# The first expert product of 39 couples as seven block products in place of eight

## The chip, the core and the metric

The kernel runs on one core of one Trainium2 chip. Its engines work side by side, each through its own list of instructions in order: TensorE (PE) for matmuls, VectorE (DVE), ScalarE (ACT), GpSimd (POOL), and SyncE (SP), which here issues most of the DMAs. POOL issues the indirect DMAs (gathers and scatters by a list of row numbers) and does tensor work between them. The metric is the device time of one execution in microseconds (us); lower is better. A change is faster or slower for us when it moves that time by more than about 0.2%.

## What is computed

A batch of 8 sequences of 2496 rows of 256 numbers passes through a filter in the frequency domain, and every row is then treated by one of eight experts. Cut to what matters:

```python
X = np.fft.rfft(x, axis=1)
Yr, Yi = Xr @ w_r - Xi @ w_i + b_r, Xr @ w_i + Xi @ w_r + b_i
Y = soft_threshold(Yr, 0.01) + 1j * soft_threshold(Yi, 0.01)
x = np.fft.irfft(Y, n=2496, axis=1).reshape(19968, 256)

e_idx = argmax(x @ w_gate)                      # one expert for each row
for e in range(8):
    h = np.maximum(x[e_idx == e] @ w1[e], 0)    # first product, 256 -> 1024
    out[e_idx == e] = gate * (h @ w2[e])        # second product, 1024 -> 256
```

The change touches the line of the first product, `x @ w1[e]`, for a part of the rows.

## The kernel before

**Numbers in two halves.** Every f32 operand of a product is kept as two f16 tensors, a high and a low part, and a product is three f16 matmuls into the same PSUM bank: high by high, high by low, low by high. So a tile of weights or tokens has an index `v` of 0 or 1, and ACT makes the high part and DVE (or POOL) the low part of each.

**Phases.** The transform runs sequence by sequence (stages called stage1, stage2, mix, inverse, stage4). Its rows go to a table `yd` in DRAM, with the gate values. Rows are sorted to experts by counting, and from then on the work is by tiles of 128 rows. Two tiles of one expert are a couple. `T_A` = 64 tiles (32 couples) come from the first four sequences; they are the first phase of the experts and overlap the last sequences of the transform. `T_2` = 78 tiles (39 couples) are the second phase, and with them, spread evenly, go `T_M` = 18 mixed tiles, each of which has 64 rows of one expert and 64 of another. `BLOCKS` holds the order of couples and mixed tiles, `SEQ` that of tiles, `POS` the place of a tile in it.

**The path of a tile.** `gathers`: POOL fetches its rows with an indirect DMA (L1485). `tokens`: DVE finds the largest value and a power of two as scale (L438 to L449, L1507), ACT makes the high part (L1512), DVE the low part (L1513); SP turns both round with a transposing DMA into `eT` (L1526). `up`: the first product, 48 matmuls for a couple in four PSUM banks of 128 x 512 (L1617). ACT writes the high part of the positive values to `hh` (L1627), DVE the low part (L1628), and the bank is free. `down`: the second product, 24 matmuls a tile (L1581). ACT scales the result (L1597), POOL scatters it to `out` with an indirect DMA (L1600).

**Weights.** They lie in DRAM (`wd`) as f16 halves, 8192 columns an expert, half for each product. `W` holds three places for couples and two for mixed tiles. `fetch` and `half_fetch` load a place when its next couple has another expert; the DMA is issued every time but has a condition, and does nothing when the expert is the same.

**What sets the order.** Nothing is scheduled on the chip. When the program is built, a planner (class `Issue`) plays all the work through as generators: `yield "P", r, d, f` asks for engine P (PE), with due time `r` and planned duration `d`, and `f` writes the instruction. A free engine takes the waiting piece with the earliest due time. `yield slots[...]` waits for a buffer, `yield "name", t` for an event. Only the order that comes out goes to the chip, engine by engine; there the engines wait for each other by semaphores. The constants at the head of the file are due times and offsets. The planner counts an indirect DMA as 1.0 us of POOL.

`blocks_` starts a `block` for each couple or mixed tile, 5.6 us of due time a tile. In `tokens`, a tile waits for the first product of the tile `AHEAD` places before it.

## Time and profile before

| | us |
|---|---|
| runs (three): median, lowest, highest | 1423.33, 1422.81, 1424.46 |
| the profiled execution, as timed | 1422.78 |
| its span, from first to last instruction | 1421.0 |
| PE, DVE, ACT, POOL busy in it | 1390.6, 986.2, 738.9, 650.5 |
| first product of couples (L1617), 3408 matmuls, busy | 389.2 |
| second product of couples (L1581), 3408 matmuls, busy | 391.0 |

[...] What a matmul costs in a row of them is the distance of their starts: the span of a group of them, from its start to the start of the next group. Rows of the profile name the line of the program, the engine, the operation, the output and the inputs by tile name, shapes, and counts. In rows of instructions in order of time the first number is the start, the second the time taken, and the bracket the idle time of that engine just before, with what ended it. In rows of stretches each engine has its busy time and its number of instructions; PEclk is the granted clock of TensorE.

### The profile page before, as it was taken

How to read it: one execution, taken by the hardware profiler on the slowest of the kernel's cores; microseconds unless marked ns; L12 is line 12 of the kernel's file. 1: busy time of each engine (PE TensorE's matmuls, PEld its weight loads, DVE VectorE, ACT ScalarE, POOL GpSimd, SP SyncE). 2: the span in 40 equal slices, each digit the busy share in tenths (PEclk: the TensorE clock that was granted, in tenths of full speed). 3: DMA queues.
4: the chain of work that ended last, by engine and by line, in shares of the span. 5: the costliest groups of instructions: out<-in, count | busy, mean ns of one | idle time of the engine just before them, and what ended most of it. 6: DMA issues, size and time to landing. Idle time of an engine off the chain costs nothing.

```text
span 1421.0 us, 40860 instructions
## 1 busy us (share of the span) xinstructions
PE 1390.6 (98%) x15696; PEld 1237.5 (87%) x15696; DVE 986.2 (69%) x2849; ACT 738.9 (52%) x1401; POOL 650.5 (46%) x733
## 2 busy tenths in 40 slices
PE   7999999999999999899999999999999999999996
PEld 5998989898988888789998888999989999999996
DVE  5888877789999888668998774555455545554541
ACT  4877687778677765343333344434444434434431
POOL 3464645564567663334455634343343334333311
PEclk9999999999999999999999999999999999999999
DMA  8699989898988898786353373554644565555440
GB/s 212 166 212 230 205 226 207 214 212 224 217 203 188 201 227 190 196 253 174 97 158 78 88 178 80 135 142 128 164 107 103 135 168 132 135 137 139 126 106 23
DMA packets 285997, 231.54 MB, mean 163 GB/s; under 512 B 239246, under 2 KB 248080, under 8 KB 279167
## 3 DMA queue, kind: packets, MB, share of 16 engines
q1 hardware_dynamic: 270377, 187.02, 54.1%
q0 software_dynamic: 15424, 41.90, 12.7%
q8 instruction: 123, 2.02, 0.6%
q14 instruction: 73, 0.60, 0.1%
HBM read 286.72 MB, written 58.52 MB: 243 GB/s over the span
## 4 chain that ended last, share of the span: by engine, by line
PE 83%; DVE 6%; issue 5%; DMA 2%; POOL 2%; ACT 1%; SPq 1%; POOLq 0%; DVEq 0%; ACTq 0%
PE ps L1617 27%; PE ps L1581 26%; PE ps L823 11%; PE ps L715 5%; PE ps L793 3%; PE ps L919 3%; PE ps L853 3%; DMA x<-in_x 1%; PE ps L964 1%; PE ps L758 1%; POOL out L1600 1%; PE ps L817 1%; PE ps L599 1%; PE ps L1385 1%; DVE z L839 1%
## 5 line engine op out<-in xcount | busy, mean ns | idle before, releaser
L1617 PE MATMUL ps<-eT,wbuf 128*128 128x256 f16 x3408 | 389.2, 273 | 3.6 <-DMA wbuf<-wd 3.6
L1581 PE MATMUL ps<-wbuf,hh 128*128 128x256 f16 x3408 | 391.0, 273 | 0.0
L1617 PEld LDWEIGHTS <-wbuf 128*128 128x128 f16 x3408 | 331.6, 98 | 43.7 <-DMA wbuf<-wd 3.8
L1581 PEld LDWEIGHTS <-hh 128*128 128x128 f16 x3408 | 329.0, 98 | 41.9 <-issue 3.8
L1628 DVE SCALAR_TENSOR_TENSOR hh<-ps,hh 128x512 f16<-128x512 f32 x284 | 196.0, 690 | 225.7 <-ACT hh L1627 224.6
L1600 POOL DMA_INDIRECT out<-o,sidx x160 | 166.0, 1038 | 372.7 <-ACT o L1597 351.6
L1627 ACT ACTIVATE hh<-ps 128x512 f16<-128x512 f32 x284 | 169.5, 597 | 231.7 <-PE ps L1617 229.8
L823 PE MATMUL ps<-whl,xt 128*128 128x256 f16 x1920 | 222.6, 273 | 0.0
L1485 POOL DMA_INDIRECT yg<-yd,gidx x160 | 158.2, 989 | 138.7 <-DVE yhl L1513 82.9
L823 PEld LDWEIGHTS <-xt 128*128 128x128 f16 x1920 | 187.8, 98 | 30.9 <-issue 0.6
L1597 ACT ACTIVATE o<-ps,facs 128x256 f32<-128x256 f32 x160 | 75.7, 473 | 178.5 <-PE ps L1581 169.3
L1512 ACT ACTIVATE yhl<-yg,ys 128x256 f16<-128x256 f32 x160 | 80.8, 506 | 66.9 <-DVE ysi L449 31.7
L715 PE MATMUL ps<-f1t,x 117*128 117x120 f32 (+1 forms) x704 | 90.3, 282 | 9.2 <-DMA x<-in_x 7.8
L715 PEld LDWEIGHTS ps<-f1t,x 117*128 117x128 f32 (+1 forms) x704 | 85.6, 197 | 12.6 <-issue 9.1
L843 POOL TENSOR_TENSOR zhl<-z,zhl 128x512 f16<-128x512 f32 x64 | 75.6, 1182 | 30.8 <-ACT zhl L841 15.4
L1513 DVE SCALAR_TENSOR_TENSOR yhl<-yg,ys,yhl 128x256 f16<-128x256 f32 x160 | 78.9, 509 | 14.1 <-ACT yhl L1512 13.9
L842 POOL CAST zhl<-z 128x512 f16<-128x512 f32 x54 | 34.1, 631 | 107.7 <-DVE z L839 76.6
L838 ACT ACTIVATE zhl<-ps,sc 128x512 f32<-128x512 f32 x80 | 54.8, 686 | 39.1 <-PE ps L823 32.1
L1122 POOL TENSOR_TENSOR wsp<-wr,wsp 128x512 f16<-128x512 f32 x58 | 70.7, 1219 | 4.8
L1628 DVE SCALAR_TENSOR_TENSOR lategt<-ps,lategt 128x512 f16<-128x512 f32 x36 | 24.8, 688 | 65.8 <-ACT lategt L1627 65.8
L839 DVE SCALAR_TENSOR_TENSOR z<-ps,zhl 128x512 f32<-128x512 f32 x80 | 54.6, 684 | 20.7 <-ACT zhl L838 19.4
L919 PE MATMUL ps<-bdt,f4t 120*117 120x512 f16 x264 | 68.8, 379 | 0.0
(236 smaller groups left out, 2113.6 us busy)
## 6 DMA issues: line engine op xcount, KB each, us to landing
wbuf<-wd SPq DMA_DIRECT2D x142, 1024.0 KB
latebt<-wd SPq DMA_DIRECT2D x36, 1024.0 KB
latebdt<-wd SPq DMA_DIRECT2D x36, 1024.0 KB
yd<-yt SPq DMA_DIRECT2D x120, 158.4 KB
x<-in_x SPq DMA_DIRECT2D x106, 156.0 KB
wr<-in_moe_w SPq DMA_DIRECT2D x32, 512.0 KB
wd<-wsp SPq DMA_DIRECT2D x64, 256.0 KB
yg<-yd,gidx POOLq DMA_INDIRECT x160
```

What stands on the lines that cost most here:

```text
L715: T.matmul(pv[:, dh, :, m * j:m * j + m], xs[:k, j0 + j, 128 * dh:128 * dh + 128], fw, start=True, stop=True)
L823: T.matmul(yp[:, 256 * j:256 * j + 256], xt_[:, v, 2 * dh + j, 64 - 64 * u:192 - 64 * u], whl[:, dh, vw, 256 * u:256 * u + 256], start=Fal ...
L919: T.matmul(pt[:P3], w, src[:, :, :, vb_], start=(n == 0), stop=(n == 2))
L1485: yield "G", r + 5.6 * POS[t] - 30, 1.0, lambda: G.indirect_dma_start(out=yg, out_offset=None, in_=src, in_offset=bass.IndirectOffsetOnAxi ...
L1512: yield "A", r - 10, 0.5, lambda: A.activation(yhl[:, 0], yg[:, :256], AF.Copy, scale=s)
L1513: yield "D", r - 10, 0.48, lambda: V.scalar_tensor_tensor(yhl[:, 1], yg[:, :256], s, yhl[:, 0], ALU.mult, ALU.subtract)
L1581: T.matmul(st["pt", t][1][c * q:c * q + c, :256], hh[:, v, fc, 128 * n + c * q:128 * n + c * q + c], wq[:, fc // 2, vw, fc % 2], start=(fc ...
L1597: yield "A", r - DN, 0.47, lambda: A.activation(o, pt[:, :256], AF.Copy, scale=fac)
L1600: yield "G", r - DN, 1.0, lambda: G.indirect_dma_start(out=outs[POS[t] % 8], out_offset=bass.IndirectOffsetOnAxis(ap=sidx[:, t:t + 1], axi ...
L1617: T.matmul(pt[:, 128 * m * j:128 * m * (j + 1)][:, 64 * q:128 * m - 64 * (len(w) - 1 - q)], wq[:, dh, g // 4, vw, 128 * (g % 4):128 * (g % ...
L1627: yield "A", r, 0.6, lambda: A.activation(hv[:, 0], pt, AF.Relu)
L1628: yield "D", r, 0.69, lambda: V.scalar_tensor_tensor(hv[:, 1], pt, 0.0, hv[:, 0], ALU.max, ALU.subtract)
```

## The change

A couple's first product is a matrix of 1024 x 256 weights by 256 x 256 tokens. Cut every matrix in four blocks by the halves of the 256 inner positions and of the 1024 and 256 outer ones. Done directly this takes eight products of a half-size block of weights (512 x 128) by a block of tokens (128 x 128): in each PSUM bank `up` ran 12 matmuls of 256 columns, that is two of these products. The change makes seven products, a form of Strassen's scheme, for the couples of the second phase (`seven(t)`: `T_A <= t < T_S`). The first phase and the mixed tiles keep `up`.

- **Sums of weights.** `sums` loads the f32 weights of the first product again for each expert, and `sums_of` makes four sums and differences of their blocks (POOL or DVE), scales and halves them (ACT; POOL or DVE), and writes them to a new DRAM table `wsd`, 4096 columns an expert. The buffers are parts of tiles that the transform has left. `sws` keeps each expert's scale for it.
- **Sums of tokens.** `presum` makes four combinations of a couple's token blocks: an addition of 512 elements, three of 256, 128 and 128, a high part (ACT) and a low part, all else on POOL.
- **Seven products.** `up7`: each has 12 matmuls of 128 columns into a PSUM bank of 128 x 512. The results are combined: the first is copied to SBUF (ACT) and added to the second (DVE), that is added to copies of the third and the fourth (`third`: ACT, then POOL), and these sums are added back into banks of four products (`leave`: DVE), from where the two halves go to `hh` as before, by ACT and DVE, and the bank is free.
- **Fetch.** `sum_fetch` loads 1 MB of sums behind the weights of the first product, under the same condition, into places `SV`.
- **Token halves.** For odd tiles of these couples the low part goes from DVE (one instruction) to POOL (two).
- **Waits.** `down` waits for "hq" (two of them, of its tile's columns) in place of "hh". `AHEAD` goes from 6 to 10.
- **Constants.** Nearly all due times and offsets have new values, P from 69.07 to 69.48, `RT` from -33.27 to -40.17; the rest is left out here. The planned size of a weight load goes from 1.05e6 to 1.4e6 bytes.

The core of the diff:

```diff
-AHEAD = 6
+AHEAD = 10
+Q7, F7, S7, D7, Q8 = 85.85, 20.22, 238.5, 1.13, 343.06
...
+    def sums_of(e, raw, r):
+        a11, a21, a12, a22 = (raw[i // 2][:, 512 * (i % 2):512 * (i % 2) + 512] for i in range(4))
+        for o, a, b, op in ((a22, a21, a22, ALU.add), (a21, a11, a21, ALU.subtract), (a11, a22, a11, ALU.subtract), (a12, a12, a11, ALU.subtract)):
+            yield either("G", r, 1.25, "D", r + Q7, 1.06, lambda g: g.tensor_tensor(o, a, b, op))
+        s = sws[:, e:e + 1]
+        for i, rv in enumerate((a22, a11, a21, a12)):
+            il = yield slots["t7"]
+            hl = late_tile("zhl", il, [128, 2, 512], F16)
+            yield "A", r, 0.72, lambda: A.activation(hl[:, 0], rv, AF.Copy, scale=s)
+            yield [("G", r, 2.04, multi(
+                       lambda: G.tensor_scalar(rv, rv, s, 1.0, ALU.mult, ALU.mult),
+                       lambda: G.tensor_tensor(hl[:, 1], rv, hl[:, 0], ALU.subtract))),
+                   ("D", r + Q7, 1.12, lambda: V.scalar_tensor_tensor(hl[:, 1], rv, s, hl[:, 0], ALU.mult, ALU.subtract))]
...
+        if seven(t) and t % 2:
+            yield "G", r - 10, 1.1, f
+        else:
+            yield "D", r - 10, 0.48, lambda: V.scalar_tensor_tensor(yhl[:, 1], yg[:, :256], s, yhl[:, 0], ALU.mult, ALU.subtract)
...
+        if seven(t):
+            io.go(presum(t, eT, r - F7))
+            yield "w", t, 2, 0
+            yield "th", t
+            yield slots["seven"]
...
+    def presum(t, eT, r):
+        ix = yield slots["x7"]
+        x = wide32(ix)
+        xq = x.rearrange("p (c m n) -> p c m n", c=2, m=2)
+        e = eT.rearrange("p m v c n -> p v c m n")
+        def f(g):
+            g.tensor_tensor(xq[:, 0], xq[:, :, 1], xq[:, 0], ALU.subtract)
+            g.tensor_tensor(xq[:, 1, 1], xq[:, 1, 1], xq[:, 0, 0], ALU.subtract)
+            g.tensor_tensor(xq[:, 1, 0], xq[:, 1, 0], xq[:, 1, 1], ALU.subtract)
+        yield "G", r, 1.2, lambda: G.tensor_tensor(xq, e[:, 0], e[:, 1], ALU.add)
+        yield "G", r, 1.5, lambda: f(G)
+        il = yield slots["t7"]
+        th = late_tile("zhl", il, [128, 2, 512], F16)
+        yield "A", r, 0.64, lambda: A.activation(th[:, 0], x, AF.Copy)
+        yield "G", r, 1.2, lambda: G.tensor_tensor(th[:, 1], x, th[:, 0], ALU.subtract)
...
+    def up7(t, w, eT, ie, hh, r):
+                for j in range(4):
+                    for n, (va, vx) in enumerate(((0, 0), (0, 1), (1, 0))):
+                        T.matmul(o[:, 128 * j:128 * j + 128], a[:, va, 128 * j:128 * j + 128], x[:, vx], start=(n == 0), stop=(n == 2))
...
+        def third(k, i, o, n):
+            ix = yield slots["x7"]
+            make(k, wide32(ix), ("x7", ix), n)
+            yield "A", r, 0.6, lambda: A.activation(u[k], o, AF.Copy)
...
+            yield "72", t
+            yield "G", r, 1.25, lambda: G.tensor_tensor(u[k], u[k], u["2"], ALU.add)
...
+        def leave(i, o, k, h, n):
+            yield "7" + k, t
...
+            yield "D", r, 0.69, lambda: V.tensor_tensor(o, o, u[k], ALU.add)
+            used7(k)
+            a = o.rearrange("p (c n) -> p c n", c=4)
+            hq = hh[:, :, 4 * h:4 * h + 4, 128 * n:128 * n + 128]
+            yield "A", r, 0.6, lambda: A.activation(hq[:, 0], a, AF.Relu)
+            yield "D", r, 0.69, lambda: V.scalar_tensor_tensor(hq[:, 1], a, 0.0, hq[:, 0], ALU.max, ALU.subtract)
+            io.free(i)
+            io.set("hq", t, h, n)
...
+        i, o = yield "P", r, 0.69, into(w[:, 0, 0], eT[:, 0, :, 0]), True
+        io.go(first(i, o))
+        i, o = yield "P", r + UP, 0.69, into(sv[1], th[:, :, 3]), True
+        io.go(second(i, o))
+        i, o = yield "P", r + UP, 0.69, into(sv[0], th[:, :, 0]), True
+        io.go(third("4", i, o, 2))
+        i, o = yield "P", r + UP, 0.69, into(sv[2], th[:, :, 1]), True
+        io.go(third("3", i, o, 1))
+        io.go(leave(i, o, "4", 1, 1))
+        i, o = yield "P", r + UP, 0.69, into(w[:, 1, 0], eT[:, 0, :, 1]), True
+        io.go(leave(i, o, "s", 0, 0))
+        i, o = yield "P", r + UP, 0.69, into(sv[3], eT[:, 1, :, 1]), True
+        io.go(leave(i, o, "4", 0, 1))
+        i, o = yield "P", r + UP, 0.69, into(w[:, 1, 1], th[:, :, 2]), True
+        io.go(leave(i, o, "3", 1, 0))
```

More of the change, by code (lines that the diff above doesn't have):

```diff
@@ L141 @@
 T1 = 0.91
[L142 to L156 removed]
+S2 = 36.83
+E1 = 58.57
+DS = 2.6
+ES = 1.78
+Z1 = 37.4
+Z2 = 11.44
+IV = -3.7
+IS = 1.99
+GO = -30.27
+R0 = 41.69
+R1, G1 = 11.46, 0.18
+GA = 0.28
+W0 = 9.34
+W1 = 29.87
+TG = 86.17
 HEAD = 15.0
@@ L1430, in open_h @@
                 io.put(slots[k + "1"], ("late", i))
+        for k, n in (("z7", 2), ("x7", 3), ("t7", 3)):
+            for i in range(n):
+                io.put(slots[k], i)
         io.set("late")
@@ L1560, in block @@
         st["nu", t] = 0
-        for half in range(2 * m):
+        if seven(t):
+            io.go(up7(t, w[0], eT, ie, hh, r))
+        for half in range(0 if seven(t) else 2 * m):
             io.go(up(t, m, half, w, eT, ie, hh, r + UP * half * (m - 1)))
@@ L1583, in down @@
         for half in range(m):
-            for i in range(2 * half, 2 * half + 2):
-                yield "hh", t0, i
+            if seven(t0):
+                yield "hq", t0, half, n
+            else:
+                for i in range(2 * half, 2 * half + 2):
+                    yield "hh", t0, i
             if half == 0:
```

157 lines of the change are left out of this document (118 added, 39 removed).

## The prediction

> **What bounds the kernel now.** I read the page first, then the chain of work that ended last, then the busy times of two stretches late in the span, cut at the chain's own boundaries.
>
> ```profile
> span 1421.0 us, 40860 instructions
> PE 1390.6 (98%) x15696; PEld 1237.5 (87%) x15696; DVE 986.2 (69%) x2849; ACT 738.9 (52%) x1401; POOL 650.5 (46%) x733
> PE 83%; DVE 6%; issue 5%; DMA 2%; POOL 2%; ACT 1%; SPq 1%; POOLq 0%; DVEq 0%; ACTq 0%
> ```
>
> TensorE is at work 98% of the span and holds 83% of the chain. A busy PE is not yet a PE at its peak, so the next question is whether its matmuls stand back to back. The chain in order of time (start, us, what) shows one period of the second phase:
>
> ```profile
> 1112.80 8.04 PE ps L1617 x144
> 1120.84 8.09 PE ps L1581 x96
> 1128.93 5.24 PE ps L1617 x48
> 1134.17 5.24 PE ps L1581 x48
> 1139.41 8.04 PE ps L1617 x144
> ```
>
> Every piece starts where the last ended. The period is 1139.41 - 1112.80 = **26.61 us**: two couples (first product L1617, 48 matmuls; second product L1581, 48 matmuls) and one mixed block. A couple is 5.24 + 5.24 = 10.48 us, and the mixed block 26.61 - 20.96 = 5.65 us. There are 39 couples and 18 mixed blocks in this phase: 18 such periods and, before them, three couples alone. The stretches show the other engines in the same period:
>
> ```profile
> core 0: us, PE busy (x) PEld busy (x) DVE busy (x) ACT busy (x) POOL busy (x), PEclk, DMA share, GB/s
> 1112.80:1139.41 26.61, 26.61 (x342) 24.05 (x339) 13.70 (x45) 10.77 (x20) 10.51 (x11) 1.00 0.51 115
> 1139.41:1166.02 26.61, 26.61 (x342) 24.06 (x339) 13.71 (x45) 10.78 (x20) 10.14 (x11) 1.00 0.59 155
> ```
>
> PE is idle nowhere, at a granted clock of 1.00. POOL has 10 or 11 instructions, all indirect DMAs (five gathers, five scatters), and is busy 10.1 us. It is the engine on which the change puts most, so its room decides.
>
> **PE: what is removed and added.** A couple's first product was 48 matmuls of 256 columns in 5.24 us, 109 ns each. It becomes 7 x 12 = 84 matmuls of 128 columns. Matmuls of that form stand in the first phase:
>
> ```profile
> 320.14 2.17 PE L853 MATMUL ps<-gt,zhl 128*128 128x128 f16 x36
> 322.15 1.46 PE L919 MATMUL ps<-bdt,f4t 120*117 120x512 f16 x6
> ```
>
> 36 of them, each with its own weight load, take 322.15 - 320.14 = 2.01 us, 56 ns each, so a product of 12 takes 0.67 us and the seven take 4.69 us. PE saves 5.24 - 4.69 = 0.55 us a couple, 39 x 0.55 = **21.5 us** in all, and a period needs 26.61 - 1.10 = 25.5 us of PE. An eighth of the arithmetic is saved, but half the columns cost 51% of the time, not 50%.
>
> **POOL: what is added.** Each couple brings nine tensor instructions: in presum an addition of 512 elements from f16, three f32 operations of 256, 128 and 128, and a 512 subtraction; in third two additions of 512 f32; in tokens a scaling and a subtraction of 256, which leave DVE for odd tiles. The nearest rows are the weight preparation and the scaled bias (minimum/median/maximum ns):
>
> ```profile
> 109.48 0.72 POOL L1119 TENSOR_SCALAR wsp<-wr,swe 128x512 f16<-128x512 f32 x1
> 110.30 0.69 POOL L1121 TENSOR_SCALAR wr<-wr,swe 128x512 f32<-128x512 f32 x1
> 111.07 1.16 POOL L1122 TENSOR_TENSOR wsp<-wr,wsp 128x512 f16<-128x512 f32 x1
> 112.20 0.70 POOL L1119 TENSOR_SCALAR wsp<-wr,swe 128x512 f16<-128x512 f32 x1
> ...
> L1122 POOL TENSOR_TENSOR wsp<-wr,wsp x58: 1153/1161/1702, 64.8 to 507.9; 128x512 f16<-128x512 f32 x58
> L657 POOL TENSOR_TENSOR b<-bs,b x16: 658/666/1023, 33.3 to 433.6; 32x256 f16<-32x256 f32 x16
> L654 POOL TENSOR_SCALAR bs<-bias,sc x8: 545/550/949, 32.2 to 431.5; 128x256 f32<-128x256 f32 x8
> ```
>
> From start to start a 512 operation of two tensors takes 112.20 - 111.07 = 1.13 us, 0.03 less than its duration; one with a scalar takes 0.08 more than its duration (110.30 to 111.07). A 256 operation is 0.63 by the same correction. One of 128 is not shown: half way on from 512 to 256 gives 0.38, an estimate. So presum is 1.08 (f16 inputs, a little under 1.13) + 0.63 + 0.38 + 0.38 + 1.13 = 3.60, third 2 x 1.13 = 2.26, tokens 0.63 + 0.63 = 1.26: **7.1 us a couple**, 14.3 a period. With durations in place of starts, and 5% for the longer ones among them, it is 15.0.
>
> The indirect DMAs cost more than their busy time:
>
> ```profile
> 1124.53 0.98 POOL L1485 DMA_INDIRECT yg<-yd,gidx  x1 [0.30 <-DVE ys L447]
> 1125.81 0.98 POOL L1485 DMA_INDIRECT yg<-yd,gidx  x1 [0.30 <-DVE yhl L1513]
> 1127.10 1.01 POOL L1600 DMA_INDIRECT out<-o,sidx  x1 [0.30 <-ACT o L1597]
> ...
> 703.33 1.01 POOL L1600 DMA_INDIRECT out<-o,sidx  x1 [0.30 <-issue]
> 704.34 0.87 POOL L1377 TENSOR_TENSOR ob<-ob,t 117x384 f16<-117x384 f16 x1
> 705.36 1.01 POOL L1485 DMA_INDIRECT yg<-yd,gidx  x1 [0.16 <-issue]
> ```
>
> Behind another indirect DMA one starts only after 0.30 us, whoever is named as releaser; behind a tensor instruction after 0.16; a tensor instruction behind it starts at once. With nine of some fourteen POOL instructions a couple being tensor ones I take a gap of 0.21, so 1.21 each, ten a period: 12.1 us (11.6 if all gaps were 0.16, 13.0 if all were 0.30). POOL then needs 14.3 + 12.1 = **26.4 us** a period, from 25.8 to 28.0, against 25.5 of PE. **POOL becomes the bound**, and its pace is almost that of before.
>
> Why this reaches PE: the second product of a couple waits for "hq", which waits for DVE's addition of u3 or u4, which third makes on POOL; and three PSUM banks are held until then. PE has the second product of the couple before and the next couple's seven in front of it, some 9.9 us. The ways out of the seven (ACT 0.6, DVE 0.69, twice) take about 3 of that, and eight banks carry only part of the rest, so POOL may run some 5 us late (estimate) before PE stands.
>
> **The sum**, against the profiled execution's own 1422.8 us (span 1421.0; the median of the runs is 1423.3, 0.5 above):
>
> ```profile
> L1600 POOL DMA_INDIRECT out<-o,sidx x160: 966/1007/1858, 553.8 to 1410.2; - x160
> L1485 POOL DMA_INDIRECT yg<-yd,gidx x160: 942/980/1218, 509.5 to 1347.9; - x160
> ```
>
> - The last gather starts 62 us before the last scatter. In these 2.3 periods POOL has no gathers and is free: PE's pace, 2.3 x -1.1 = -2.5 us.
> - The other 15.7 periods go at POOL's pace: 15.7 x (26.4 - 26.61) = -3.3 us (from -12.7 to +21.8).
> - The three couples ahead: POOL 7.1 + 4 x 1.21 = 11.9 against 10.48, 3 x 1.4 = +4.3, which the 5 us of room take up: 0.
> - One us for boundaries, such as the first fetch of the sums: +1.
>
> 1422.8 - 2.5 - 3.3 + 1 = **1418 us**: of 21.5 us saved on PE some 5 are left.
>
> **What I cost at nothing, and its cover.** DVE gets five additions of 0.69 (L1628's row below) and loses one 0.48 a couple: 13.7 + 5.9 = 19.6 of 26 us. ACT gets three copies of 0.6 and one of 0.64: 10.8 + 4.9 = 15.7.
>
> ```profile
> L1628 DVE SCALAR_TENSOR_TENSOR hh<-ps,hh 128x512 f16<-128x512 f32 x284 | 196.0, 690 | 225.7 <-ACT hh L1627 224.6
> L1627 ACT ACTIVATE hh<-ps 128x512 f16<-128x512 f32 x284 | 169.5, 597 | 231.7 <-PE ps L1617 229.8
> SPq L1526 <- DVE yhl L1513: 176.8, 49, 7.8
> ```
>
> An added wait stands at the head of DVE: leave waits for third, and behind it queue the token scales, whose transposes are not due for several us. SP gets one or two more DMAs a couple behind the fetch of the weights, whose wait they share; SP waits 176.8 us for token work anyway, and DMA is 0.5 to 0.6 busy. The changed start times only reorder a first phase that PE fills.
>
> The sums of the weights themselves need, on POOL, 8 x 4 x (1.13 + 0.77 + 1.13) = 97 us, between the transform's end and the second phase. There is this room:
>
> ```profile
> 700.00:800.00 100.00, 99.66 (x971) 89.60 (x968) 89.64 (x276) 38.15 (x73) 55.39 (x57) 1.00 0.44 115
> 800.00:900.00 100.00, 99.48 (x922) 88.98 (x920) 64.11 (x209) 40.54 (x76) 43.12 (x44) 1.00 0.54 137
> ```
>
> POOL is free for about 101 us, less some 15 for the gaps, and DVE, which may take them too, for 46: cover enough.
>
> **Rivals.**
> *PE's pace after all.* If POOL keeps within 25.5 us a period the whole 21.5 us stays: 1401 us. It asks for 1.2 us less than my count, below the low end of 25.8. For it speak POOL's work done ahead (gathers and presums run up to three couples early).
>
> *The two engines get in each other's way: slower.* DVE's L1513 reads two tensors of SBUF, and once a period a scatter meets it:
>
> ```profile
> 1122.88 0.48 DVE L1513 SCALAR_TENSOR_TENSOR yhl<-yg,ys,yhl 128x256 f16<-128x256 f32 x1
> 1122.99 1.24 POOL L1600 DMA_INDIRECT out<-o,sidx  x1 [6.42 <-ACT o L1597]
> ```
>
> It took 1.24 us, not 1.01. Now POOL idles between such meetings; when it never idles, each of the three L1513 left a period (two of even tiles, one mixed) can hold it for up to 0.48: 1.4 us a period, 15.7 x 1.4 = 22, so 1440 us at the full price and 1429 at half. It decides from 0.3 us a period on, where the gain of 5 us is gone. Against it: the gaps of 0.16 to 0.30 can take part of a meeting. [...]
>
> *The sums come late.* They are due from about 754 us on (P x 8 + RT + S7), with the first seven at some 885. If only 60% of the room above counts they miss it by about 15 us, and PE, whose order is fixed, waits: 1433.
>
> *Nothing gained or lost.* 0.1 to 0.4 us a period more on POOL gives 1420 to 1426.
>
> **The numbers.** POOL's pace with part kept (1409 to 1420): 0.32. PE's pace (1400 to 1409): 0.15. Given back entirely, within 0.2%, about what a measurement of this kernel can tell from no change: 0.18. Meetings on the port, or POOL at its upper prices (1426 to 1440): 0.25. Late sums or worse: 0.10. So faster 0.47, same 0.18, slower 0.35. The range leaves out the best part of PE's pace and the worst of the last two: 1403 to 1437.
>
> **What would show it.** L1617's 128-column matmuls of the seven at 56 ns; POOL over 95% busy in stretches of the second phase, against 39% now; idle PE there whose releaser is DVE's addition or, behind it, POOL's third; a period near 26.4 us. I am wrong if PE is still gapless there (then 1401), if POOL's instructions are longer than their rows, or if PE's gap is a single one at the first seven (late sums).

## The result, and the profile after

The changed kernel takes **1549.84 us** (median of four runs, 1544.76 to 1560.41) where the kernel before took 1423.84 in the same session (1422.81 to 1424.46): a ratio of 1.0887, 95% interval 1.0856 to 1.0918. The forecast was 1418, within 1403 to 1437. It was wrong in sign and, by 132 us, in size.

The page of the profiled execution (1550.53 us, span 1548.7) has these in the place of the three lines that the prediction began with:

```profile
span 1548.7 us, 44764 instructions
PE 1411.6 (91%) x17102; PEld 1255.5 (81%) x17102; DVE 1211.1 (78%) x3035; ACT 829.9 (54%) x1592; POOL 1038.4 (67%) x1151
PE 12%; POOL 9%; DVE 8%; issue 6%; DMA 5%; ACT 2%; SPq 0%; POOLq 0%; ACTq 0%; DVEq 0%
```

In the chain that ended last PE held 83% of the span. Now the shares sum to 42%, so the chain could be followed back over less than half of the span, and of these 42 PE has 12; the rest is scattered over POOL, DVE, DMA and others. A chain that changes engine all the time is a chain of waits, not of one full engine: POOL is busy for 67% of the span, and for 75 to 89% in the second phase, where I had made it the bound. Stretches of the second phase show the same (columns as in the prediction):

```profile
1000.00:1100.00 100.00, 89.74 (x1390) 83.92 (x1388) 73.51 (x179) 48.66 (x95) 81.57 (x90) 0.95 0.46 119
1100.00:1200.00 100.00, 91.22 (x1334) 83.50 (x1332) 85.57 (x181) 49.52 (x97) 88.67 (x98) 0.97 0.45 120
1200.00:1300.00 100.00, 81.00 (x1227) 75.58 (x1225) 65.56 (x156) 42.86 (x83) 74.85 (x84) 0.91 0.58 145
```

PE is idle for 9 to 19 of 100 us and its granted clock is 0.91 to 0.97, against gapless work at 1.00 before.

**Where the time went.** I cut each span at two starts of matmuls and one end: the first product of the first couple, the first product of the 33rd couple (where the second phase begins), and the end of the last second product. The groups of the changed kernel's matmuls, with their first and last start, give the cuts at 541.3, 951.7 and (1536.9 and a fifth of a us) 1537.1:

```profile
L1701 PE MATMUL ps<-eT,wbuf x1536: 269/273/421, 541.3 to 946.4; 128*128 128x256 f16 x192
L1758 PE MATMUL ps<-eT,wbuf x936: 219/219/314, 951.7 to 1528.8; 128*128 128x128 f16 x188
L1662 PE MATMUL ps<-wbuf,hh x3408: 270/273/421, 553.8 to 1536.9; 128*128 128x256 f16 x190
```

| us | ahead of the experts | first phase | second phase |
|---|---|---|---|
| before | 532.9 | 363.3 | 513.1 |
| after | 541.3 | 410.4 | 585.4 |
| difference | +8.4 | +47.1 | +72.3 |

So there are two large losses, and only one of them lies where the seven products are. PE's waits by releaser show that they are two different things. First the first phase with its transform (560 to 951 us), then the second phase (950 us to the end); columns: total, times, longest:

```profile
PE ps L1389 <- DVE ob L1381: 18.3, 17, 3.7
PE ps L1389 <- POOL ob L1381: 10.0, 7, 4.4
...
PE ps L1701 <- DMA lategt<-yhl: 36.2, 12, 7.2
PE ps L1662 <- ACT hh L1810: 14.1, 9, 3.9
PE ps L1662 <- DVE hh L1811: 12.6, 18, 2.0
```

In the first phase PE waits in the routing matmuls (L1389) for products that DVE and POOL make. In the second it waits for transposed tokens of the mixed tiles, which take no part in the seven at all, and for the ways out of the seven. The kernel before had from 533 us on hardly more than 3.6 us of waits named (`PE ps L1617 <- DMA wbuf<-wd`).

**The ring of waits.** The waits of the other engines in the second phase say why tokens came late:

```profile
POOL xt L1737 <- DMA eT<-yhl: 34.4, 9, 8.4
...
DVE ps L1806 <- POOL xt L1798: 55.3, 18, 6.1
...
SPq L1528 <- PE ps L1662: 90.0, 32, 9.6
SPq L1600 <- DVE ps L1806: 55.7, 15, 8.7
SPq L1600 <- POOL yhl L1582: 39.7, 14, 7.8
```

Read them in a circle. POOL stands at a token sum (L1737) until a transpose has landed; behind it in POOL's list are third (L1798), the low parts of odd tiles (L1582) and the gathers. DVE stands at leave (L1806) until third is done; behind it are the token scales and low parts. SP stands at a transpose (L1600) until DVE's or POOL's part of it is done; before it in SP's list are weight fetches (L1528) that wait for PE. (The row of 55.7 names L1806, the leave just ahead in DVE's list; the seven longest of these waits end 0.03 us after the low part, L1587, that stands behind it.) And PE waits for the transpose. Every engine is in order, so whoever waits holds up work that another needs.

One part of it, in order of time, all engines (start, us, what; in brackets the idle time before and its releaser):

```profile
1227.80 2.55 DVE L1574 SCALAR_TENSOR_TENSOR facs<-yg,ysi,isb 128x1 f32<-128x1 f32 x1
1228.04 1.19 POOL L1742 TENSOR_TENSOR zhl<-xt,zhl 128x512 f16<-128x512 f32 x1
1228.16 0.58 ACT L1793 ACTIVATE xt<-ps 128x512 f32<-128x512 f32 x1
1229.15 1.17 POOL L1737 TENSOR_TENSOR xt<-eT 128x512 f32<-128x512 f16 x1
1230.28 1.34 DVE L1587 SCALAR_TENSOR_TENSOR yhl<-yg,ys,yhl 128x256 f16<-128x256 f32 x2
1231.68 1.22 SPq L1600 DMA_TRANSPOSE lategt<-yhl  x1
1233.79 2.51 POOL L1798 TENSOR_TENSOR xt<-xt,z 128x512 f32<-128x512 f32 x2
1235.12 0.70 DVE L1806 TENSOR_TENSOR ps<-ps,xt 128x512 f32<-128x512 f32 x1 [3.50 <-POOL xt L1798]
1236.83 0.37 PE L1701 MATMUL ps<-lategt,latebt 128*128 128x64 f16 x4 [5.74 <-DMA lategt<-yhl]
```

A DVE operation on one element a partition, of which the like took 0.22 us on average in the second phase of before (L1507), takes 2.55: it ends at 1230.35, and two operations of POOL that began after it (1228.04 and 1229.15) are over at 1230.32. The low part behind it ends at 1231.62, the transpose is issued at 1231.68, and PE starts when it has landed at 1236.83, after 5.74 us of nothing. Meanwhile third's first copy was ready at 1228.74 (1228.16 + 0.58), but its additions stand behind the next couple's token sum and begin at 1233.79, so DVE waits 3.50 us more. The rows that follow in the trace close the ring:

```profile
1242.74 0.34 SPq L1528 DMA_DIRECT2D latebt<-wd  x1
1243.18 4.25 SPq L1600 DMA_TRANSPOSE eT<-yhl  x2
1251.97 1.16 POOL L1737 TENSOR_TENSOR xt<-eT 128x512 f32<-128x512 f16 x1 [8.38 <-DMA eT<-yhl]
1255.56 2.51 POOL L1798 TENSOR_TENSOR xt<-xt,z 128x512 f32<-128x512 f32 x2
1256.89 0.70 DVE L1806 TENSOR_TENSOR ps<-ps,xt 128x512 f32<-128x512 f32 x1 [5.77 <-POOL xt L1798]
1257.50 0.87 DVE L1587 SCALAR_TENSOR_TENSOR yhl<-yg,ys,yhl 128x256 f16<-128x256 f32 x1
1258.40 1.22 SPq L1600 DMA_TRANSPOSE lategt<-yhl  x1
1261.63 0.50 PE L1701 MATMUL ps<-lategt,latebt 128*128 128x64 f16 x6 [4.63 <-DMA lategt<-yhl]
```

PE's mixed tile came late, so SP stands 7.8 us at a weight fetch that waits for PE's matmuls of that tile, and the two transposes behind it go out at 1243.18. POOL stands 8.38 us for one of them at its token sum; behind that come a gather, a scatter and third. DVE stands 5.77 us for third, the low part of the next mixed tile is right behind, its transpose goes out 0.03 us after that has ended, and PE stands again for 4.63 us. Of PE's twelve waits for a mixed tile five, 19.4 of the 36.2 us, come from a low part right behind a leave that had waited for third.

After this pause PE also ran slowly:

```profile
1236.80:1240.80 4.00, 3.97 (x64) 0.50 0.64 261
1214.00:1218.00 4.00, 4.00 (x98) 1.00 0.49 118
```

(PE alone: stretch, length, busy and count, PEclk, DMA share, GB/s.) For four us the granted clock is 0.50; after the wait of 4.63 us it was 0.50 too (1261.60 to 1265.60). The waits named in the second phase sum to some 66 us (36.2 + 14.1 + 12.6 and 3.3 of smaller ones). At full clock and without a gap PE would have needed 513.1 - 21.5 = 491.6; 585.4 - 491.6 - 66 leaves some 28 us. The granted clock of the whole phase,

```profile
951.70:1537.10 585.40, 518.23 (x7766) 476.87 (x7764) 420.04 (x958) 275.92 (x530) 467.86 (x515) 0.96 0.49 126
```

lacks 0.04 of 585, so the slow clock is at most some 23 us of these 28 (an estimate).

The eight kernels e4 to e11 below ran beside a kernel before that itself took 1455.4 or 1457.9 us, an excess of which the second phase of e7 (eight products, 513.2 us, no wait) shows nothing. Read these eight by the lengths of their parts and by the named waits, not by their ratios. PE also stands in them for some time with no wait named, at most 0.8 us a phase in the other kernels; it is given beside.

### The profile page after: what moved, and what is told of

Its sections match the earlier page's. It is cut to its first block, busy times and chain, and to the rows that moved or that the text cites. A ratio compares the mean times of both kernels' runs of the same rounds, so it can differ in the third digit from the quotient of the medians.

```text
span 1548.7 us, 44764 instructions
## 1 busy us (share of the span) xinstructions
PE 1411.6 (91%) x17102; PEld 1255.5 (81%) x17102; DVE 1211.1 (78%) x3035; ACT 829.9 (54%) x1592; POOL 1038.4 (67%) x1151
## 5 line engine op out<-in xcount | busy, mean ns | idle before, releaser
L1662 PE MATMUL ps<-wbuf,hh 128*128 128x256 f16 x3408 | 420.4, 276 | 28.4 <-ACT hh L1810 14.1
L1662 PEld LDWEIGHTS <-hh 128*128 128x128 f16 x3408 | 327.1, 99 | 76.8 <-DVE hh L1811 19.6
L1701 PE MATMUL ps<-eT,wbuf 128*128 128x256 f16 x1536 | 181.3, 277 | 11.0 <-DMA wbuf<-wd 7.4
L1701 PEld LDWEIGHTS <-wbuf 128*128 128x128 f16 x1536 | 151.1, 99 | 33.3 <-DMA wbuf<-wd 8.4
L1806 DVE TENSOR_TENSOR ps<-ps,xt 128x512 f32<-128x512 f32 x117 | 79.7, 693 | 70.3 <-POOL xt L1798 55.3
L1811 DVE SCALAR_TENSOR_TENSOR hh<-ps,hh 128x512 f16<-128x512 f32 x156 | 103.8, 683 | 22.0 <-ACT hh L1810 20.4
L1712 DVE SCALAR_TENSOR_TENSOR hh<-ps,hh 128x512 f16<-128x512 f32 x128 | 87.1, 684 | 40.7 <-ACT hh L1711 40.4
L1798 POOL TENSOR_TENSOR xt<-xt,z 128x512 f32<-128x512 f32 x78 | 99.2, 1283 | 10.7 <-ACT xt L1793 9.8
L846 POOL TENSOR_TENSOR zhl<-z,zhl 128x512 f16<-128x512 f32 x68 | 80.8, 1188 | 36.0 <-ACT zhl L844 33.2
L1587 DVE SCALAR_TENSOR_TENSOR yhl<-yg,ys,yhl 128x256 f16<-128x256 f32 x121 | 86.4, 720 | 18.1 <-ACT yhl L1579 12.0
L1574 DVE SCALAR_TENSOR_TENSOR facs<-yg,ysi,isb 128x1 f32<-128x1 f32 x160 | 88.4, 553 | 5.6
```

The lines of the kernel that those rows point to most:

```text
L1574: V.scalar_tensor_tensor(fac, yg[:, 256:257], si, route["is"][:, t:t + 1], ALU.mult, ALU.mult)
L1587: yield "D", r - 10, 0.48, lambda: V.scalar_tensor_tensor(yhl[:, 1], yg[:, :256], s, yhl[:, 0], ALU.mult, ALU.subtract)
L1662: T.matmul(st["pt", t][1][c * q:c * q + c, :256], hh[:, v, fc, 128 * n + c * q:128 * n + c * q + c], wq[:, fc // 2, vw, fc % 2], start=(fc ...
L1701: T.matmul(pt[:, 128 * m * j:128 * m * (j + 1)][:, 64 * q:128 * m - 64 * (len(w) - 1 - q)], wq[:, dh, g // 4, vw, 128 * (g % 4):128 * (g % ...
L1798: yield "G", r, 1.25, lambda: G.tensor_tensor(u[k], u[k], u["2"], ALU.add)
L1806: yield "D", r, 0.69, lambda: V.tensor_tensor(o, o, u[k], ALU.add)
```

## The experiments

Eighteen kernels, each timed beside the kernel before. Parts are cut as above. The expectations weigh three explanations: *ports* (DVE's operations with two SBUF inputs are held up by POOL's tensor work; the word is a name only, no run shows a port), *POOL queue* (POOL simply has too much work) and *loop* (the engines wait for each other in the order of their lists). They call POOL GpSimd and DVE VectorE.

| kernel | median us | ratio to before [95%] | ahead | first | second |
|---|---|---|---|---|---|
| e0_order | 1437.89 | 1.0093 [1.0074, 1.0111] | 543.2 | 367.9 | 513.1 |
| e1_sums | 1479.02 | 1.0369 [1.0349, 1.0390] | 544.4 | 409.1 | 513.1 |
| e2_seven | 1507.88 | 1.0572 [1.0550, 1.0594] | 541.7 | 371.6 | 584.8 |
| e3_fac | 1549.17 | 1.0879 [1.0847, 1.0911] | 542.2 | 410.5 | 583.0 |
| e4_third_dve | 1542.58 | 1.0567 [1.0532, 1.0602] | 539.9 | 413.7 | 576.6 |
| e5_noport | 1551.17 | 1.0653 [1.0625, 1.0682] | 539.7 | 414.4 | 578.5 |
| e6_presum_late | 1587.60 | 1.0895 [1.0863, 1.0926] | 540.3 | 413.3 | 619.4 |
| e7_sums_dve | 1485.74 | 1.0199 [1.0171, 1.0228] | 541.2 | 417.8 | 513.2 |
| e8_replan | 1563.84 | 1.0751 [1.0718, 1.0785] | 541.7 | 412.7 | 594.8 |
| e9_replan_third | 1506.87 | 1.0341 [1.0310, 1.0372] | 546.9 | 411.6 | 537.2 |
| e10_sums_after | 1472.25 | 1.0115 [1.0089, 1.0141] | 543.5 | 378.5 | 533.2 |
| e11_third | 1481.99 | 1.0170 [1.0143, 1.0196] | 542.2 | 378.3 | 548.7 |
| e12_pe_alone | 1433.57 | 1.0066 [1.0049, 1.0083] | 540.7 | 369.9 | 507.2 |
| e13_load_alone | 1456.36 | 1.0219 [1.0202, 1.0236] | 542.2 | 371.1 | 530.2 |
| e14_cut_tokens | 1532.36 | 1.0765 [1.0743, 1.0787] | 541.3 | 409.8 | 566.8 |
| e15_no_presum | 1451.51 | 1.0183 [1.0159, 1.0206] | 543.6 | 371.4 | 525.4 |
| e16_presum_unread | 1513.12 | 1.0609 [1.0576, 1.0642] | 546.3 | 370.8 | 583.6 |
| e17_presum_alone | 1471.98 | 1.0343 [1.0323, 1.0363] | 543.3 | 369.7 | 545.0 |

### The change in three parts

**Order alone.** No couple takes seven products, no sums are made; the new constants, `AHEAD` and planned sizes stay.

```diff
     def seven(t):
-        return T_A <= t < T_S
+        return False
...
-    io.go(sums(P * B + RT + S7))
```

> The changed kernel with its new constants and its order, but with the eight products of before for all couples and without the sums of weights (nothing is left out of the computation). Theory ports: VectorE's instructions with two SBUF inputs wait for GpSimd's tensor instructions, so what GpSimd was given is the cause, and this run is within 1415 to 1435 us. Theory POOL queue: GpSimd simply has too much work of its own; the same 1415 to 1435 us. Theory order: the retuned due times are at fault; 1480 us or more.

The second phase is that of before to the tenth of a us, but 10.3 us are lost ahead of the experts and 4.6 in the first phase. That is a little over the range of the first two explanations, and far under that of the third, order.

**Order and sums.** The first part alone of that edit: the sums of weights are made and nothing reads them.

> As e0_order, but the sums of weights are made and written to DRAM, and nothing reads them. Theory ports: the stretch from 600 to 950 us loses what it lost in the changed kernel, 1455 to 1490 us in all, with VectorE's two-input instructions of the routing (0.45 to 0.52 us before) at 0.7 us or more. Theory POOL queue: GpSimd is busy about 79% of that stretch with room left, so at most 1440 us.

The first phase grows by 409.1 - 367.9 = 41.2 us, and PE has the same waits in L1389 (18.1 and 9.2 us) as the changed kernel. Two stretches, first without the sums, then with them:

```profile
700.00:800.00 100.00, 99.21 (x966) 89.06 (x964) 94.74 (x275) 36.76 (x71) 50.77 (x52) 1.00 0.40 112
800.00:900.00 100.00, 99.81 (x934) 89.52 (x933) 73.39 (x246) 39.85 (x77) 44.20 (x44) 1.00 0.45 122
```

```profile
700.00:800.00 100.00, 87.25 (x792) 75.52 (x791) 90.88 (x222) 37.88 (x70) 78.20 (x73) 0.95 0.68 188
800.00:900.00 100.00, 89.83 (x817) 78.14 (x815) 95.66 (x235) 40.04 (x74) 80.59 (x74) 0.97 0.55 156
```

POOL took on 27 and 36 us, and DVE is busy for 91 and 96% with fewer instructions than it had (222 for 275 and 235 for 246): its operations became longer. Two groups of the routing's two-tensor operations on DVE between 600 and 900 us show it (line, operation, names, shapes, count, busy, mean ns). Without the sums:

```profile
L1359 DVE TENSOR_TENSOR ol<-t,rlo 117x512 f16<-117x512 f16 (+1 forms) x48 | 29.8, 621 | 0.7 <-PE ps L1389 0.6
L1381 DVE TENSOR_TENSOR ob<-ob,t 117x384 f16<-117x384 f16 (+1 forms) x18 | 8.7, 485 | 0.1
```

With them:

```profile
L1359 DVE TENSOR_TENSOR ol<-t,rlo 117x512 f16<-117x512 f16 (+1 forms) x48 | 39.2, 817 | 1.3 <-PE ps L1389 1.3
L1381 DVE TENSOR_TENSOR ob<-ob,t 117x384 f16<-117x384 f16 (+1 forms) x31 | 26.3, 849 | 0.1
```

The 48 operations of L1359 take 817 ns in place of 621. (In the kernel before they took 453, so the new order alone had made them longer, at a cost of 4.6 us of first phase at most.) And the planner, which may give L1381 to either engine, moved 13 of these multiplications from the fuller POOL to DVE, where each takes 849 ns in place of 485: L1381 on DVE is what PE waits for, 18.1 us.

**Seven products without sums.** `sums` is not run, and the fetch reads halves of `wd` of the same size in place of `wsd`.

```diff
-                    yield "sums"
...
-                nc.sync.dma_start(a, wsd[ds(f, 1), :, 1024 * i:1024 * (i + n)]...
+                nc.sync.dma_start(a, wd[ds(f, 1), :, 4096 + 1024 * i:4096 + 1024 * (i + n)]...
...
-    io.go(sums(P * B + RT + S7))
```

> The changed kernel without the sums of weights: the seven products read other halves of the weights in their place, so that part of the output is other numbers; loads, products and all else are kept. Theories ports and POOL queue both: the second phase starts some 45 to 65 us earlier than in the changed kernel and is as long as there (about 585 us), so 1480 to 1505 us. If the two losses depend on each other: 1520 us or more, or below 1470.

The second phase is 584.8 us, that of the changed kernel, and the first is nearly that of the order alone; the time is 3 us over the range. So the parts add up: 14.9 for the order, 41.2 for the sums and 584.8 - 513.1 = 71.7 for the seven make 127.8; the spans differ by 1548.7 - 1421.0 = 127.7.

### The sums of weights

**On DVE alone.** Order and sums, with `sums_of`'s tensor work given to DVE.

```diff
-            yield either("G", r, 1.25, "D", r + Q7, 1.06, lambda g: g.tensor_tensor(o, a, b, op))
+            yield "D", r, 0.7, lambda: V.tensor_tensor(o, a, b, op)
...
-            yield [("G", r, 2.04, multi(
...
+            yield "D", r, 0.75, lambda: V.scalar_tensor_tensor(hl[:, 1], rv, s, hl[:, 0], ALU.mult, ALU.subtract)
```

> As e1_sums (eight products, sums made and not read), but all tensor work of the sums except the high parts is on VectorE: 32 additions and 32 low parts, some 45 us, and GpSimd gets none of the 97 us. Theory ports: the routing's two-input instructions go back to 0.5 to 0.62 us, and the time is 1440 to 1460. If VectorE's fullness and not the meeting with GpSimd is what costs: 1470 us or more.

If meetings of the two engines were all, this should have helped. The first phase is 417.8 us, of which PE stands 7.0 with no wait named: the stall moved. From 800 to 900 us DVE is 89% busy, and PE is at 65% and waits up to 9.1 us for a low part of `hh` that stands behind sums and routing on DVE:

```profile
PE ps L1659 <- DVE hh L1709: 15.8, 3, 9.1
PE ps L1389 <- POOL ob L1381: 15.6, 9, 2.4
```

**After the routing.** Order and sums, with the sums held back until the routing is over.

```diff
     def sums(r):
         yield "late"
+        yield "tiles", 1
```

> As e1_sums (eight products, sums made on GpSimd and not read), but the sums start only when the routing of the second phase is done, so that they meet no routing work. Theory ports: GpSimd's sums cost because VectorE's two-input routing instructions meet them; now 1437 to 1455 us. If the amount of work or of DMA is what costs: 1465 to 1480 as in e1_sums.

The first phase falls to 378.5 us, 30.6 less than with the sums in the routing, and of PE's waits in L1389 there, 18.1 us for DVE and 9.2 for POOL, only 1.5 for POOL is left. So the sums cost the first phase so much because they stand beside the routing, which needs DVE and POOL for its own pace. But the second phase, into which most of them now fall, rises by 20.1, and PE waits there 10.4 us for weights (`wbuf`): two thirds of the gain are lost again.

### The second phase: single repairs

**The token scale with one tensor input.** The operation that took 2.55 us above gets one tensor input and two scalars.

```diff
-            V.scalar_tensor_tensor(fac, yg[:, 256:257], si, route["is"][:, t:t + 1], ALU.mult, ALU.mult)
+            V.tensor_scalar(fac, yg[:, 256:257], si, route["is"][:, t:t + 1], ALU.mult, ALU.mult)
```

> The changed kernel with one instruction a tile in another form: the factor of a tile (128 x 1) is made by a tensor-scalar instruction with two scalars in place of one with two SBUF tensors; the numbers are the same. Theory ports: that instruction falls from 0.55 us in the mean to below 0.2, and the kernel gains 10 to 40 us (1510 to 1540). Theory POOL queue: GpSimd's work is the same, and the time stays within 5 us of 1550.

It takes 273 ns on average in the second phase, from 750, and hardly anything is gained (583.0): the wait moves to the next operation with two tensor inputs, L1587, whose mean goes from 911 to 1083 ns.

**No such operation at all.** The same, and the low parts of even and mixed tiles go to ACT, as a plain scaled copy with no subtraction, so that DVE has none left with two inputs from SBUF in this phase.

```diff
+        elif t >= T_A:
+            yield "A", r - 10, 0.5, lambda: A.activation(yhl[:, 1], yg[:, :256], AF.Copy, scale=s)
```

> The changed kernel without any VectorE instruction of two SBUF inputs in the second phase: the factors as in e3_fac, and the low part of tokens made by ScalarE as a plain scaled copy (so that part of the output is other numbers: the low part is the value and not the rest). Theory ports: token work is no longer held up, and the waits of TensorE on the transposed tokens of mixed tiles (36 us) mostly go: 1495 to 1525. Theories POOL queue and loop: GpSimd's list is the same, 1535 to 1555.

578.5: 7 us of 72, or 12 without the 4.9 us in which PE stands with no wait named. The meetings are real, but without them the ring is nearly as slow.

**Third on DVE.** Third's addition reads the bank itself, on DVE, and POOL loses 78 additions, 99 us.

```diff
+            yield "72", t
...
-            yield "A", r, 0.6, lambda: A.activation(u[k], o, AF.Copy)
+            yield "D", r, 0.69, lambda: V.tensor_tensor(u[k], o, u["2"], ALU.add)
...
-            yield "G", r, 1.25, lambda: G.tensor_tensor(u[k], u[k], u["2"], ALU.add)
```

> The changed kernel with the two additions of third on VectorE, straight from the PSUM bank (0.69 us each), in place of a copy by ScalarE and an addition by GpSimd (1.28 us each). GpSimd has 2.6 us a couple less, 100 us in all, VectorE 1.4 us more. Theory POOL queue: GpSimd's amount of work sets the second phase, so most of 39 x 1.7 us comes back: 1485 to 1510 us. Theory ports: two of nine tensor instructions of GpSimd are gone, so a fifth of the loss: 1530 to 1545. Theory loop (engines that wait for each other in the order of their lists, with GpSimd's third in front of VectorE's token work): 1500 to 1530, with VectorE's waits on GpSimd gone.

576.6: 9 us of 72, or 22 without the 13.7 us with no wait named, with POOL busy 68% in place of 83% (1000 to 1400 us). The relieved POOL only waits longer at the token sums, for the transposes:

```profile
POOL xt L1737 <- DMA eT<-yhl: 74.4, 21, 7.9
```

So POOL's load by itself is not the bound; the kernels under "The second phase taken apart" show the same.

**Token sums later.** `F7` from 20.22 to 8.0: the sums stand later in POOL's list, behind more gathers.

> The changed kernel with presum due 8 us ahead of its couple in place of 20. Theory loop: GpSimd reaches presum after its tokens have landed, so its 38 us of waits for the transposed tokens fall below 15, and 15 to 45 us come back (1505 to 1535). Theory POOL queue: the work is the same, within 8 us of 1550. Theory ports: the same, within 8 us.

619.4, 34 us worse (7.1 of them with no wait named). POOL's waits for transposes at the token sum hardly fall (28.0 us from 34.4), so the loop's range was missed too, and PE's largest wait is now for weights (`PE ps L1662 <- DMA wbuf<-wd: 40.8, 7, 11.3`, from the waits of PE): another arc of the ring.

**A plan with measured durations.** The planner's durations are set to those of the profile: indirect DMAs 1.25 in place of 1.0, the low part on DVE 0.8 for 0.48, scales 1.1 for 0.83, POOL's low part 1.25 for 1.1, three token sums 1.75 for 1.5, and transposed tokens land 2 us later.

```diff
-            yield "G", r + 5.6 * POS[t] - 30, 1.0, lambda: G.indirect_dma_start(out=yg, ...
+            yield "G", r + 5.6 * POS[t] - 30, 1.25, lambda: G.indirect_dma_start(out=yg, ...
...
-        yield TAIL
+        yield TAIL + 2.0
```

> The changed kernel, same work, with an order planned from durations nearer to those measured in it: indirect DMAs 1.25 us of GpSimd in place of 1.0, presum's three small operations 1.75 for 1.5, token halves on GpSimd 1.25 for 1.1, token scales 1.1 for 0.83 and low parts 0.8 for 0.48 on VectorE, and 2 us more until a transposed tile has landed. Theory loop: the engines wait for each other because the order was planned too tight, and 20 to 50 us of the second phase come back. Theory POOL queue: the amount of work is what it was, less than 10 us come back. To be read by the length of the second phase (577 us in the changed kernel from the first to the last of the seven products' L1758 starts) beside the time.

594.8, or 583.1 without the 11.7 us with no wait named: nothing came back. The wait for transposes is gone from POOL (4.1 us from 34.4) and from PE (1.9 from 36.2), and PE waits instead for the ways out (20.9 and 16.7) and for weights (15.2).

**Both.** The new plan and third on DVE together.

> e8_replan and e4_third_dve together: third on VectorE from PSUM, and the order planned from the measured durations. If order and GpSimd's load both matter, the second phase (567 us in e4_third_dve) is below 540 us; theory POOL queue: below 540 too; if neither does, 560 to 570.

537.2: 48 us of 72 come back, where the one gave 9 and the other took 9; without the time with no wait named (14.6 us here) it is 63, where the one gave 22 and the other 2. So there are two knots on POOL, the token sum that waits for a transpose and third that stands behind it, and each alone suffices to hold PE.

**A third of the couples.** Seven products without sums, for 13 of the 39 couples (`t // 2 % 3 == 0`).

> As e2_seven (no sums; the seven read other halves of the weights, so that part of the output is other numbers), but only every third couple has the seven products, 13 of 39. If each couple of seven costs the same, a third of e2_seven's 70 us over e0_order: 1458 to 1465 us. If the loss comes from fullness (GpSimd's work per period of 26.6 us falls to about 17 us): PE's gain of 0.55 us a couple shows, 1428 to 1438 us.

548.7, but no engine's work is named by PE's waits there, only 23 us in 43 short pieces with no wait named. The run is inconclusive on the ring.

### The second phase taken apart

All of these leave out the sums of weights, as the run with the seven alone (584.8) does, but for the cut token chain.

**PE and the ways out alone.**

```diff
-            io.go(presum(t, eT, r - F7))
...
-        i, o = yield "P", r + UP, 0.69, into(sv[1], th[:, :, 3]), True
+        i, o = yield "P", r + UP, 0.69, into(sv[1], eT[:, 1, :, 0]), True
...
-            yield "G", r, 1.25, lambda: G.tensor_tensor(u[k], u[k], u["2"], ALU.add)
...
-        if seven(t) and t % 2:
+        if False:
```

> The kernel with seven block products and no sums of weights (the run with the seven alone), less all that the seven add on POOL: the token sums are left out (the seven read tokens as they stand), so are third's two additions (ACT's copies stay), and the low part of the odd tiles goes back to DVE. PE's seven products, the three copies of ACT and DVE's five additions on the way out stay. If my term for PE was right (0.55 us a couple) and the loss comes from what was put on POOL, the second phase falls from 584.8 us to 488-500 and the whole to some 1417-1425 by the undisturbed time of before (ratio 0.995-1.001). If the products of 128 columns or the way out over ACT and DVE cost PE the time, the second phase stays above 530.

507.2, outside the 488 to 500 that I had set, but under 513. Two whole periods of it:

```profile
1113.97:1139.48 25.51, 25.48 (x408) 24.09 (x409) 18.93 (x54) 12.93 (x25) 10.08 (x11) 1.00 0.35 77
1139.48:1164.99 25.51, 25.51 (x412) 24.12 (x410) 20.09 (x56) 14.01 (x27) 10.02 (x11) 1.00 0.84 244
```

A period is **25.51 us** with PE gapless: PE's term was 25.5. What is missing to 491.6 are three waits for a mixed tile's tokens, 11.1 us, and the slow clock behind them (granted 0.98 and 0.97 from 1200 to 1300 and to 1400 us, 1.00 in the two hundreds ahead of these).

**The load alone.** Eight products, and beside them the POOL work of the seven, which nothing reads.

```diff
+        if T_A <= t < T_S:
+            io.go(presum(t, eT, r - F7))
+            io.go(unread(t, r))
...
+    def unread(t, r):
+        yield "hh", t, 0
+        yield "th", t
...
+        for _ in range(2):
+            yield "G", r, 1.25, lambda: G.tensor_tensor(u, x[:, 0], x[:, 1], ALU.add)
```

> The kernel with eight products and the new order (no seven, no sums of weights), and beside it the POOL work of the seven, made and read by nothing in the product: the token sums with their ACT copy, two additions of 512 f32 a couple, the low part of the odd tiles on POOL. [...] If the load fits and only its place in the couple's chain costs (PE waits for the results), the second phase stays within 513-525.

530.2, 17 us over the 513 without this work and 5 over the range. Two periods:

```profile
1220.10:1247.60 27.50, 26.86 (x339) 23.93 (x338) 20.46 (x44) 10.94 (x23) 24.99 (x29) 1.00 0.28 70
1342.60:1370.00 27.40, 26.78 (x338) 23.91 (x336) 20.36 (x44) 10.72 (x23) 24.93 (x29) 1.00 0.50 148
```

POOL is busy 25.0 of 27.5 us, and gaps of at most 0.4 us ahead of the indirect DMAs fill most of the rest (29.0 us in 146 of them from 910 to 1410 us, 1.6 a period): this is POOL's own pace, what I had priced at 26.4. Here the token sums never stand for a transpose. A full POOL whose new work nobody reads costs 17 us.

**Token sums left out, left unread, and alone.** Three kernels make a square. Without the sums, third stays on POOL (the first two parts of the edit of PE alone):

> The kernel with the seven alone (no sums of weights), less the token sums (the seven read tokens as they stand); third's additions, the low part of odd tiles on POOL and the ways out stay. [...] If the token sums are what breaks the phase, the second phase falls from 584.8 to 500-515. If third, which lies inside the couple's own chain, is what breaks it, 550 or more stay.

With the sums made as they were, but not read by PE (the second part alone):

> The run with the seven alone (no sums of weights), in which the token sums are made on POOL as before but PE does not read them: the seven read tokens as they stand. The load on POOL and DVE and the order of the queues are those of the run with the seven alone (second phase 584.8 us); only PE's dependence on the token sums is gone. Without the token sums at all the phase took 525.4. If the load is what costs, 565 or more stay; if PE's wait for the sums (and through it SP's and POOL's waits for PE) is what costs, the second phase falls to 525-540.

With the sums made and read, but no third and no low parts on POOL (the last two parts):

> The run in which nothing of the seven was left on POOL (second phase 507.2 us), with the token sums put back, and read by PE: third's additions stay left out and the low part of odd tiles stays on DVE. POOL has 3.6 of the 7.1 us a couple. If PE's dependence on the token sums is harmful by itself, the second phase rises to 550 or more; if it is harmful only on a POOL that is full, it stays within 507-525.

| second phase, us | no token sums | token sums on POOL |
|---|---|---|
| no third, no low parts on POOL | 507.2 | 545.0 |
| third and low parts on POOL | 525.4 | 584.8 (583.6 unread) |

Third and low parts alone cost 18, the token sums alone 38, both 78. Of the 78, POOL's own pace is worth at most 530.2 - 507.2 = 23. And whether PE reads the token sums is, with third there, worth 1 us: PE does not wait for them. What they do harm to stands behind them in POOL's list. POOL's waits in the kernel with token sums alone (545.0, between its two expectations), where it is busy only 64%, show it at the sum's first instruction 23 times:

```profile
POOL xt L1736 <- DMA eT<-yhl: 82.7, 23, 8.2
```

**The token chain cut.** The changed kernel, in which the transposes of the second phase read a constant table, so they wait for no token work.

```diff
-        yield from move(r - 10, 1.4e5, 1.2, lambda: nc.sync.dma_start(eT..., yhl..., transpose=True))
+        if t >= T_A:
+            src = t16[:, :512].rearrange("p (v d) -> p v d", v=2)
+        else:
+            src = yhl
+        yield from move(r - 10, 1.4e5, 1.2, lambda: nc.sync.dma_start(eT..., src..., transpose=True))
```

> The changed kernel with one dependence cut: in the second phase the transposing DMAs read a constant table in place of the tokens' high and low parts, so they no longer wait for POOL's, ACT's and DVE's token work (which is all still made); everything else as it was. If the token chain (gather, scales on DVE, parts, transpose) is what PE waits for, the waits of L1701 for the mixed tiles' tokens go and the second phase falls from 585 to 525 or less. If it is one of several chains on the same full engines, it gains under 25 us and other waits (for hh, hq, the weights) take its place.

566.8, a gain of 19, and the waits for the ways out grow to 19.9 and 17.8. Cutting one arc leaves the others.

**What is shown and what stays open.** Shown: the three losses add up; PE's saving is there; a full POOL whose new work nobody reads costs 17 us; token sums on POOL cost 38 without third and 59 with it, and with it whether or not PE reads them; the ring is closed once in the rows above (1231 to 1262 us), and five of PE's twelve waits for mixed tiles pass through third and leave; removing DVE's operations with two SBUF inputs gains 2 (the token scale alone) to 7 us, 12 at most. Argued from the waits, and borne out by the replan with third on DVE, but not isolated: that it is this ring (third behind the token sum, leave behind third, token scales and low parts behind leave, transposes behind these and behind weight fetches) that turns 18 and 38 into 78, and that the 38 are the waits at the token sum and not its 3.6 us of work. Not found: why the new constants cost 10 us ahead of the experts, and an order in which the change gains. None of these kernels is faster than the kernel before; even with nothing of the seven on POOL and no sums the ratio is 1.0066.

## Why the prediction was wrong, step by step

**PE's term was right.** "A period needs 26.61 - 1.10 = 25.5 us of PE": 25.51.

**POOL's price was a little low, and not the failure.** I said 26.4, "from 25.8 to 28.0"; alone it is 27.4 to 27.5. Tensor operations were longer than their rows: third's 512 addition, which I priced at 1.13, has a mean of 1283 ns in the changed kernel, and the 256 one of the token sums, which I priced at 0.63 from a row of 32 partitions, takes 0.80 from start to start (L1733 at 1223.61, the next at 1224.41).

```profile
L1798 POOL TENSOR_TENSOR xt<-xt,z 128x512 f32<-128x512 f32 x78 | 99.2, 1283 | 10.7 <-ACT xt L1793 9.8
```

With 27.45 in place of 26.4 the same sum gives 15.7 x 0.84 - 2.5 + 1 = +12 us, 1434 and still inside the range; the load alone took 17, where the changed kernel took 127.

**The step that failed is "What I cost at nothing, and its cover".** There I wrote of the wait at the head of DVE that "behind it queue the token scales, whose transposes are not due for several us", and of SP that it "waits 176.8 us for token work anyway". I had named the queue and then let it go on the word "several", at a cost of 0. DVE stood 55.3 us at that head, SP 55.7 for the low parts behind it, POOL 34.4 behind SP's transposes, and PE 36.2 behind those; the second phase grew by 72 us where the sum had it shrink. I also never asked what POOL's own new head waits for: token sums read transposed tokens, so POOL, which fetches the tokens, now waits for them. The sum took the largest of the engines' loads for the period; that holds only where the queues between them have slack, and here the lists form a ring.

**"Cover enough" failed for the sums of weights.** I counted free time on POOL (101 us, less 15) and on DVE (46). The sums did fit there, by time; they were not late. But the routing's DVE operations (L1359) went from 621 to 817 ns beside them, 13 of its multiplications moved from POOL to DVE, and PE's order has the routing's matmuls in it: 41 us. The sums also took POOL 109 us (43.4 + 26.5 + 38.8 in e1) where I had 97. My rival "the sums come late", 1433, had the right part of the change and the wrong mechanism.

**"The changed start times only reorder a first phase that PE fills" failed** by 15 us, 10.3 of them ahead of the experts.

**The rival of the two engines in each other's way had the direction wrong, and its price was no cause.** I had DVE hold POOL, 1.4 us a period. It is DVE whose operations became longer: 2.55 us for one of which the like took 0.22 before, while third's 78 additions on POOL kept within 1255 to 1311 ns, median 1282. The chances call this rival "Meetings on the port". No run shows a port, or what decides which engine is held; what the trace shows is that the 2.55 us reach over two POOL instructions, 1.19 and 1.17 and back to back, which both began after DVE's. Taking away all such operations of DVE gained 7 us, 12 at most.

**The marks I had named.** The seven's matmuls (L1758 in the changed kernel) are at their 56 ns: twelve take 0.67 us from start to start (1254.15, 1254.83, 1255.50), though the profile records 219 ns for one, so neighbours overlap in it. POOL over 95% busy: no, 75 to 89%. Idle PE behind DVE's addition and third: yes in part (DVE's additions wait 55.3 us for third), but the largest wait of PE is for transposed tokens, which I had not listed.

## What to carry to other kernels

Load per period says whether work fits, not whether it arrives: when work moves to an engine that also fetches the inputs (gathers here), write down what each engine's new head of queue waits for, and follow it until it comes back to the same engine or ends; a ring without slack cost 72 us here, where the load alone cost 17. Free time on an engine beside a stage that paces PE through the same engines is not free (41 us here). And when single repairs gain nothing, try them in pairs: two knots in one ring hide each other.

## What the runs showed of the hardware

- DVE's operations with two SBUF inputs became longer beside POOL's tensor work: on one element a partition (L1574, 87 of them in the second phase) the mean was 750 ns where its like took 220 before, and one of them took 2.55 us, over two POOL instructions; with one tensor input in its place (e3) the mean was 273. Operations of DVE from PSUM kept their length beside the same POOL: leave's mean is 693 ns, and L1811's 683 where its like took 691 before.
- A pause of PE cost twice: after 5.74 us idle its granted clock was 0.50 for the next four us, after 4.63 us idle 0.50 too, and over the second phase, at a mean of 0.96, at most some 23 us went that way (an estimate from 0.04 of 585).
